# Four edits to a fused attention and expert kernel: transfers and value scaling issued earlier, weight sums on another engine, the last stage's head prepared in the stage before, decay factors computed on the chip

## The chip, the cores and the metric

The kernel runs on one core of a Trainium2 chip. The time is the device time of one execution in microseconds (us). Within the core five engines run side by side, each with its own instruction list in program order: TensorE (PE in the profile), VectorE (DVE), ScalarE (ACT), GpSimd (POOL) and SyncE (SP, which here only issues transfers; ACT issues some as well). Sixteen DMA engines move the data. An engine whose next instruction waits also holds everything that stands behind it in its list.

## The reference, cut to what matters

```python
# attention with a decaying state; B, H, S, D = 4, 8, 768, 64
for t in range(S):
    state = gamma * state + einsum('bhd,bhe->bhde', k[:, :, t], v[:, :, t])
    y[:, :, t] = scale * einsum('bhd,bhde->bhe', q[:, :, t], state)
x = y.transpose(0, 2, 1, 3).reshape(3072, 512)
# first expert block, 512 -> 1024 -> 512
x = ((x @ w1) * (x @ w2)) @ w3 @ w_out
# second expert block, 512 -> 768 -> 512
h = maximum(maximum(x @ u1, x @ u2), x @ u3)
out = h @ u_out
```

The weights are float64 values in memory: the host passes them on as 64-bit words, and the chip decodes them.

## The kernel before, in words

**Attention.** The sequence is cut into 24 chunks of 128 positions (`seq`; two batches take turns, so chunks i and i+2 belong to the same batch, except that chunks 0, 1, 12 and 13 begin a batch and 10, 11, 22 and 23 end one). A chunk is 1 MB, loaded by SP in two halves (`load_half(i, 0)`: q and k by feature; `load_half(i, 1)`: k and v by token) into one of four buffers `ck`, so the load of chunk i+4 can be issued only when chunk i is done with. In iteration i PE does the state product of chunk i (`attn_in`, L311), the scores of chunk i+1 (L303), the value product of chunk i (`attn_av`, L320) and its state update (`attn_st`, L331). POOL multiplies the values by a decay (`scale_v`, L293) before the value product may run. DVE masks the scores into `a` (L304), which the value product reads, and multiplies the result by the output decay `gout` (`attn_ev`, L340), which frees the bank that the state product of chunk i+2 writes. ACT copies the state out of its bank (L335) for the state product of chunk i+2.

**Weights beside it.** Over iterations 2 to 21 a `Spread` deals out jobs, two ticks an iteration: eight weight tiles of 512 KB are decoded, and then `weights` makes seven operands from them. One decode is: transfer into a staging buffer (`fetch`, L85), ACT (L116), POOL (L118), DVE (L139, L141), ACT (L148), DVE (L133). Three transfers are issued by SP in iterations 0 and 1 (`more()`), the other five by ACT, each behind the decode step that frees its staging buffer (`due_more`). `weights` rounds a matrix (ACT, L204), subtracts (DVE, L205), and forms four sums and differences on POOL (L207, L208, L209, L211). The same `weights` prepares operands five more times in the expert stages, once 1024 and four times 768 wide.

**Transfers share eight completion semaphores.** They are handed out in turn, in the order of the program text, whichever engine issues; a transfer is issued only when the one eight before it has landed.

**Expert stages.** Every product is done by a seven-product scheme for 2x2 blocks (`ORDER`, q = 0 to 6), each product with its operand split into a high and a low part (`op_split`, L229 on ACT and L230 on DVE). Stage one (L464 to L466) runs in blocks of seven products; at its third block `wgen(q)` also runs `weights`. The merge (L574 to L576), the stage hj (L694 to L696, 9 blocks) and the last stage (L753 to L755) follow. For the last stage, `quad_o(n)` names the four buffers of block n of its input, `o_load` fills them, `o_pre` forms differences in place (L626 to L631) and `o_split` splits (L639 on ACT, L640 on DVE). Before, hj's last block loads three quarters of block 0 at q = 3 and 5 and the fourth at q = 6 (into `C`, which hj uses until q = 5), splits operand 0 at q = 5, and operand 1 and `o_pre(2)` come behind the stage.

Of the kernel before, what the change touches and what calls it, by code (L numbers as in the profile page):

```python
# [15 lines left out]
P = 128  # L16
B, H, S, D = 4, 8, 768, 64
NP = H // 2
C = 128
# [26 lines left out]
@with_exitstack  # L46
def fused_kernel(ctx: ExitStack, tc: tile.TileContext, ck, w12, w3t, wo1, w123, wo2, mask, gout, kdec, out):
    nc = tc.nc
# [31 lines left out]

    def fetch(src, raw, hi=None, lo=None):
        k = stage_turn[0]
        stage_turn[0] += 1
        st = stg[k % NSTG][:, :]
        (nc.scalar if late[0] else nc.sync).dma_start(out=st.bitcast(I64), in_=src)  # L85
        loaded.append((st, dec_t[k % 2][:, :], raw, hi, lo))
# [3 lines left out]
    def more(k=1):  # L90
        if k > 1:
            due[0] = 0
        for _ in range(k):
            if wq:
                wq.pop(0)()
# [101 lines left out]
    def weights(raw, n, slot=wslot):  # L197
        tmp = s_t[:, :n]

        def emit(q):  # L200
            r0, r1, r2, r3 = raw
            src = (r0, r1, r0, r2, tmp, r3, r1)[q]
            w = slot(q, n)
            nc.scalar.copy(out=w[:, 0], in_=src)  # L204
            nc.vector.tensor_tensor(out=w[:, 1], in0=src, in1=w[:, 0], op=ALU.subtract)  # L205
            if q == 0:
                nc.gpsimd.tensor_tensor(out=tmp, in0=r2, in1=r3, op=ALU.add)  # L207
                nc.gpsimd.tensor_tensor(out=r2, in0=r2, in1=r0, op=ALU.subtract)  # L208
                nc.gpsimd.tensor_tensor(out=r0, in0=tmp, in1=r0, op=ALU.subtract)  # L209
            elif q == 2:  # L210
                nc.gpsimd.tensor_tensor(out=r1, in0=r1, in1=r0, op=ALU.subtract)  # L211

        return emit
# [48 lines left out]
    kdec_sb = a_pl.tile([P, CPB, H], F32, name="kdec")  # L262
    a_pl.tile([P, 8], F32, name="pad_a")

# [42 lines left out]
    def attn_in(i):  # L307
        t, y = cks(i), y_bank(i)
        if seq[i][1]:
            for p in range(NP):  # L310
                nc.tensor.matmul(y[:, p, :], st_sb[i % 2][:, p, :], t[:, 0, p * C:(p + 1) * C],  # L311
                                 start=p == 0, stop=False, skip_group_check=True)
# [30 lines left out]

    def fetch_w12(i, u):
        raw = wraw_t[0][:, :].rearrange("p (q i n) -> p q i n", q=4, i=GA)
        fetch(w12[i, u], raw[:, 2 * u:2 * u + 2, i % GA, :])

# [11 lines left out]
    with tc.manual_schedule():  # L359
        load_half(0, 0)  # L360
        nc.sync.dma_start(out=mask_sb, in_=mask)
        load_half(0, 1)
        nc.sync.dma_start(out=kdec_sb, in_=kdec)
        load_half(1, 0)
        load_half(1, 1)
        nc.sync.dma_start(out=gout_sb[:, 0], in_=gout[:, 0])
        for b in range(2):
            nc.gpsimd.memset(st_sb[b], 0.0)
        wq += [lambda i=i, u=u: fetch_w12(i, u) for i in range(GA) for u in range(2)]
        load_half(2, 0)  # L370
        load_half(2, 1)
        nc.sync.dma_start(out=gout_sb[:, 1:2], in_=gout[:, 1:2])
        load_half(3, 0)
# [8 lines left out]
        side = Spread([step] * (4 * GA) + [drain] + [lambda q=q: wgen(q) for q in (0, 1, 5, 2, 3, 4, 6)], 2 * (last - 3))  # L382
        for i in range(last + 1):
            attn_in(i)
            if i:
                scores(i + 1)
            if i > 1:
                side.tick()
            attn_av(i)
            scale_v(i + 2)  # L390
            attn_st(i)
            if not i:
                scores(i + 1)
            attn_ev(i)
            if i > 1:
                side.tick()
            load_half(i + 4, 0)
            if i < 2:
                more()
                if i == 1:  # L400
                    more()
                    nc.sync.dma_start(out=gout_sb[:, 2:], in_=gout[:, 2:])
            load_half(i + 4, 1)
            if i == last - 2:
                op_split(0, quad_b(0)(0, 0))
# [199 lines left out]
        def quad_o(n):  # L605
            if n % 2:
                raw = (wraw_t[0][:, :1536], wraw_t[0][:, 1536:], m_a[:, :1536], w_t[6][:, :1536].bitcast(F32))
            else:
                raw = [work[nm][:, :1536] for nm in "TEUC"]
            return lambda k, e: raw[2 * e + k]  # L610
# [31 lines left out]
        for j in range(GH):  # L642
# [16 lines left out]
            for n in range(NB):  # L659
# [3 lines left out]
                for q in range(7):  # L663
# [14 lines left out]
                    if j == GH - 1 and n == NB - 1:  # L678
                        if q == 3:
                            o_load(0, 0, 0)  # L680
                            o_load(0, 0, 1)
                        elif q == 5:
                            o_split(0)
                            o_load(0, 1, 0)
                        elif q == 6:
                            o_load(0, 1, 1)
                    which, first = ORDER[q]
# [48 lines left out]
        o_sets = [[bank[k] for k in (2, 3, 0, 1)], bank[4:8]]  # L736
        o_split(1)
        o_pre(2)
        for s in range(7 * NB):
# [92 lines left out]
```

## Time and profile before

| | us |
|---|---|
| median of 3 runs (lowest to highest) | 863.97 (860.59 to 864.65) |
| the profiled execution: its time | 863.8 |
| its span, first to last instruction | 862.0 |
| PE busy | 840.9 (98%) |
| DVE busy | 589.1 (68%) |
| ACT busy | 363.8 (42%) |
| POOL busy | 190.2 (22%) |

How to read it: attention takes the first 102.8 us of the span, the expert stages the rest. A profile row of an instruction group gives its start, its length, the engine, the line, what is written from what, and in brackets how long the engine stood idle before it and what seems to have released it. PE's granted clock was 0.999 of full speed.

### The profile page before, as it was taken

Reading aid. Unit: us, or ns where it says so; the run is one execution under the profiler, and the core shown is the slowest. Engines: PE = TensorE matmul, PEld = TensorE weight load, DVE = VectorE, ACT = ScalarE, POOL = GpSimd, SP = SyncE. Lnnn points to the kernel's source line nnn. Section 1 sums busy time; section 2 is a strip of 40 time slices with the busy share of each in tenths; the row PEclk is TensorE's granted clock in tenths of the full one; section 3 lists DMA queues with packets and bytes.
Section 4 is the critical chain, followed back from the end, with each engine's and each line's share of the span. In section 5 each row is a group of like instructions: output and inputs, shape, how many; then the busy total and the mean of one; then the engine's idle time right before and its main releaser. Section 6 shows DMA issues by size and latency. Waiting matters only on the chain.

```text
span 862.0 us, 12688 instructions
## 1 busy us (share of the span) xinstructions
PE 840.9 (98%) x4938; PEld 716.6 (83%) x4938; DVE 589.1 (68%) x716; ACT 363.8 (42%) x564; POOL 190.2 (22%) x148
## 2 busy tenths in 40 slices
PE   8887999999999999999999999999999999999998
PEld 7877888887888888888888878888888888889998
DVE  2788959899475757663375768677655675688783
ACT  1423453644335353543454444453333344335542
POOL 2437415174130313100110231240003013000000
PEclk9999999999999999999999999999999999999999
DMA  8997467967979886462386599929998899873422
GB/s 331 379 401 263 149 265 263 374 244 277 382 276 357 302 309 251 139 244 97 110 313 261 179 370 400 381 98 367 421 347 306 328 367 329 296 270 145 178 99 99
DMA packets 54781, 236.34 MB, mean 274 GB/s; under 512 B 6208, under 2 KB 6336, under 8 KB 39360
## 3 DMA queue, kind: packets, MB, share of 16 engines
q1 hardware_dynamic: 37440, 132.23, 39.9%
q10 hardware_dynamic: 17280, 103.29, 32.5%
q8 instruction: 39, 0.64, 0.3%
q14 instruction: 22, 0.18, 0.1%
HBM read 163.14 MB, written 72.35 MB: 273 GB/s over the span
## 4 chain that ended last, share of the span: by engine, by line
PE 79%; DMA 8%; DVE 6%; issue 3%; ACT 1%; POOL 1%; SPq 0%; ACTq 0%; POOLq 0%; DVEq 0%
PE bank L694 9%; PE bank L695 8%; PE bank L696 8%; PE bank L465 7%; PE bank L466 7%; PE bank L464 7%; PE bank L576 4%; PE bank L575 4%; PE bank L574 4%; DMA ck<-in_ck_dram 4%; PE bank L755 3%; PE bank L754 3%; PE bank L753 3%; PE bank L515 2%; PE bank L513 2%
## 5 line engine op out<-in xcount | busy, mean ns | idle before, releaser
L694 PE MATMUL bank<-op,w 128*128 128x512 f32 x360 | 140.4, 390 | 0.6 <-ACT U L699 0.3
L696 PE MATMUL bank<-op,w 128*128 128x512 f32 x360 | 140.1, 389 | 0.0
L695 PE MATMUL bank<-op,w 128*128 128x512 f32 x360 | 140.1, 389 | 0.0
L118 POOL TENSOR_SCALAR dec<-dec 128x512 f32<-128x512 f32 x64 | 49.5, 774 | 392.9 <-ACT dec L116 369.4
L465 PE MATMUL bank<-op,w 128*128 128x512 f32 x336 | 130.9, 389 | 1.4 <-DVE op L230 1.4
L464 PE MATMUL bank<-op,w 128*128 128x512 f32 x336 | 130.9, 390 | 0.2 <-DVE U L471 0.2
L466 PE MATMUL bank<-op,w 128*128 128x512 f32 x336 | 130.8, 389 | 0.0
L694 PEld LDWEIGHTS bank<-op,w 128*128 128x128 f32 x360 | 67.6, 188 | 15.9 <-issue 1.3
L696 PEld LDWEIGHTS bank<-op,w 128*128 128x128 f32 x360 | 67.6, 188 | 14.2
L695 PEld LDWEIGHTS bank<-op,w 128*128 128x128 f32 x360 | 67.6, 188 | 13.9
L465 PEld LDWEIGHTS bank<-op,w 128*128 128x128 f32 x336 | 63.1, 188 | 14.9 <-DVE op L230 1.8
L574 PE MATMUL bank<-op,w 128*128 128x512 f32 x192 | 74.7, 389 | 0.0
L575 PE MATMUL bank<-op,w 128*128 128x512 f32 x192 | 74.7, 389 | 0.0
L576 PE MATMUL bank<-op,w 128*128 128x512 f32 x192 | 74.7, 389 | 0.0
L464 PEld LDWEIGHTS bank<-op,w 128*128 128x128 f32 x336 | 63.1, 188 | 13.8 <-issue 0.8
L466 PEld LDWEIGHTS bank<-op,w 128*128 128x128 f32 x336 | 63.1, 188 | 13.1
L148 ACT ACTIVATE dec<-stg 128x512 int32<-128x512 uint32 x64 | 43.0, 671 | 65.9 <-DVE stg L141 60.9
L116 ACT ACTIVATE dec<-stg 128x512 f32<-128x512 f32 x64 | 42.4, 663 | 41.6 <-DMA stg<-in_w_dram 17.5
L755 PE MATMUL bank<-wo,w 128*128 128x256 f32 x192 | 54.4, 283 | 1.0 <-DVE w L640 1.0
L754 PE MATMUL bank<-wo,w 128*128 128x256 f32 x192 | 54.3, 283 | 0.0
L753 PE MATMUL bank<-wo,w 128*128 128x256 f32 x192 | 54.3, 283 | 0.0
L139 DVE TENSOR_SCALAR dec<-dec 128x512 int32<-128x512 int32 x64 | 35.2, 550 | 24.6 <-POOL dec L118 24.6
(177 smaller groups left out, 1646.7 us busy)
## 6 DMA issues: line engine op xcount, KB each, us to landing
op<-opsp ACTq DMA_DIRECT2D x77, 1024.0 KB, 7.7
opsp<-op SPq DMA_DIRECT2D x25, 1024.0 KB, 6.0
ck<-in_ck_dram SPq DMA_DIRECT2D x48, 512.0 KB, 8.7
opsp<-w SPq DMA_DIRECT2D x14, 1024.0 KB, 5.7
stg<-in_w_dram ACTq DMA_DIRECT2D x19, 512.0 KB, 6.4
stg<-in_w3t_dram ACTq DMA_DIRECT2D x16, 512.0 KB, 3.5
hsp<-m SPq DMA_DIRECT2D x32, 256.0 KB, 7.4
stg<-in_w_dram SPq DMA_DIRECT2D x15, 512.0 KB, 9.5
```

The source lines that it names most:

```text
L464: nc.tensor.matmul(ps, wh, x[:, 0, k, :], start=first and k == 0, stop=False, skip_group_check=True)
L465: nc.tensor.matmul(ps, wh, x[:, 1, k, :], start=False, stop=False, skip_group_check=True)
L466: nc.tensor.matmul(ps, wl, x[:, 0, k, :], start=False, stop=k == 1, skip_group_check=True)
L574: nc.tensor.matmul(ps, wh, x[:, 0, k, :], start=kk == 0 and k == 0, stop=False)
L575: nc.tensor.matmul(ps, wh, x[:, 1, k, :], start=False, stop=False)
L576: nc.tensor.matmul(ps, wl, x[:, 0, k, :], start=False, stop=kk == 3 and k == 1)
L694: nc.tensor.matmul(ps, wh, x[:, 0, k, :], start=first and k == 0, stop=False, skip_group_check=True)
L695: nc.tensor.matmul(ps, wh, x[:, 1, k, :], start=False, stop=False, skip_group_check=True)
L696: nc.tensor.matmul(ps, wl, x[:, 0, k, :], start=False, stop=k == 1, skip_group_check=True)
L753: nc.tensor.matmul(ps, xh[:, k, o], wh[:, k], start=first and k == 0, stop=False, skip_group_check=True)
L754: nc.tensor.matmul(ps, xh[:, k, o], wl[:, k], start=False, stop=False, skip_group_check=True)
L755: nc.tensor.matmul(ps, xl[:, k, o], wh[:, k], start=False, stop=k == 2, skip_group_check=True)
```

## The change

Four edits. (1) In attention `scale_v(i + 2)` moves from behind the value product to the head of iteration i; `kdec` and `mask` are loaded by ACT's queue; all eight weight transfers are issued by SP, in iterations 0, 1, 3, 5, 6, 8, 10 and 11, between the two halves of a chunk's load. The first five go into free room in `xr2` (attention writes that tile from iteration 13 on), the others into the three staging buffers. (2) The sums in `weights` run on DVE, and two of them move from q = 0 to q = 1. (3) Block 0 of the last stage gets other buffers, is loaded at q = 3 and 4 of hj's last block, and operand 1 and `o_pre(2)` are done at q = 6 of it. (4) Only the first of six slices of `gout` is loaded (256 KB in place of 1.5 MB), with a small table `gch`; ACT makes the other five by scaling, four instructions a slice.

```diff
-        nc.sync.dma_start(out=mask_sb, in_=mask)
+        nc.scalar.dma_start(out=kdec_sb, in_=kdec)
...
-        nc.sync.dma_start(out=kdec_sb, in_=kdec)
+        nc.scalar.dma_start(out=mask_sb, in_=mask)
...
-        nc.sync.dma_start(out=gout_sb[:, 0], in_=gout[:, 0])
-        wq += [lambda i=i, u=u: fetch_w12(i, u) for i in range(GA) for u in range(2)]
+        room = xr_t[2][:, :, :, :].rearrange("p k e n -> p (k e n)")
+        home = [room[:, z * 1024:z * 1024 + 1024] for z in (0, 1, 2, 3, 0)] + [None] * 3
+        early = [lambda k=k: fetch_w12(k // 2, k % 2, home[k]) for k in range(2 * GA)]
-        nc.sync.dma_start(out=gout_sb[:, 1:2], in_=gout[:, 1:2])
+        nc.sync.dma_start(out=gout_sb[:, 0], in_=gout)
+        nc.sync.dma_start(out=gch_sb, in_=gch)
...
         for i in range(last + 1):
+            scale_v(i + 2)
             attn_in(i)
...
             attn_av(i)
-            scale_v(i + 2)
             attn_st(i)
...
             load_half(i + 4, 0)
-            if i < 2:
-                more()
-                if i == 1:
-                    more()
-                    nc.sync.dma_start(out=gout_sb[:, 2:], in_=gout[:, 2:])
+            if i in (0, 1, 3, 5, 6, 8, 10, 11):
+                early.pop(0)()
+            if i % 2 == 0 and i // 2 + 1 < CPB:
+                for n in range(NP):
+                    nc.scalar.activation(out=gout_sb[:, i // 2 + 1, n], in_=gout_sb[:, 0, n], func=ACT.Copy,
+                                         scale=gch_sb[:, i // 2 + 1, n:n + 1])
             load_half(i + 4, 1)
...
             if q == 0:
-                nc.gpsimd.tensor_tensor(out=tmp, in0=r2, in1=r3, op=ALU.add)
-                nc.gpsimd.tensor_tensor(out=r2, in0=r2, in1=r0, op=ALU.subtract)
-                nc.gpsimd.tensor_tensor(out=r0, in0=tmp, in1=r0, op=ALU.subtract)
+                nc.vector.tensor_tensor(out=tmp, in0=r2, in1=r3, op=ALU.add)
+            elif q == 1:
+                nc.vector.tensor_tensor(out=r2, in0=r2, in1=r0, op=ALU.subtract)
+                nc.vector.tensor_tensor(out=r0, in0=tmp, in1=r0, op=ALU.subtract)
             elif q == 2:
-                nc.gpsimd.tensor_tensor(out=r1, in0=r1, in1=r0, op=ALU.subtract)
+                nc.vector.tensor_tensor(out=r1, in0=r1, in1=r0, op=ALU.subtract)
...
-                raw = [work[nm][:, :1536] for nm in "TEUC"]
+                raw = (work["T"][:, :], wraw_t[0][:, 1536:], work["U"][:, :1536], wraw_t[0][:, :1536])
...
+                        elif q == 4:
+                            o_load(0, 1, 0)
+                            o_load(0, 1, 1)
                         elif q == 5:
                             o_split(0)
-                            o_load(0, 1, 0)
                         elif q == 6:
-                            o_load(0, 1, 1)
+                            o_split(1)
+                            o_pre(2)
...
-        o_split(1)
-        o_pre(2)
```

**Place 1, SP in the middle of attention.** Before, SP's list holds only the loads of the chunks there (`ck_97` to `ck_99` and `ck_96` are the four buffers); the names behind "waits" are the semaphores of transfers (DMAHW) and engines. The weight transfers stand in ACT's list.

```order
L274 DMA ck_96<-in_ck_dram 128x1024 [waits DMAHW2_49,PE_49,Pool_49]
L274 DMA ck_97<-in_ck_dram 128x1024 [waits DMAHW3_49,PE_49]
L274 DMA ck_97<-in_ck_dram 128x1024 [waits DMAHW5_49,PE_49,Pool_49]
L274 DMA ck_98<-in_ck_dram 128x1024 [waits DMAHW6_49,DMAHW4_49,PE_49]
L274 DMA ck_98<-in_ck_dram 128x1024 [waits DMAHW7_49,PE_49,Pool_49]
```

Now, from the load of the same chunk on (`xr_95` is the room in `xr2`):

```order
L276 DMA ck_96<-in_ck_dram 128x1024 [waits DMAHW0_49,PE_49,Pool_49]
L276 DMA ck_97<-in_ck_dram 128x1024 [waits DMAHW1_49,PE_49]
L85 DMA xr_95<-in_w_dram 128x512 [waits DMAHW2_49]
L276 DMA ck_97<-in_ck_dram 128x1024 [waits DMAHW3_49,PE_49,Pool_49]
L276 DMA ck_98<-in_ck_dram 128x1024 [waits DMAHW4_49,PE_49]
L85 DMA xr_95<-in_w_dram 128x512 [waits DMAHW5_49,DVE_49]
L276 DMA ck_98<-in_ck_dram 128x1024 [waits DMAHW6_49,PE_49,Pool_49]
```

Before, the third row waits for semaphore 5, which the fourth weight transfer carries, issued from ACT's list; now the weight transfers stand in SP's own list, and the eighth transfer before any of these is one that SP issued itself.

**Place 2, DVE in iterations 15 to 17.** `w_65`, `w_66`, `w_70` and `w_67` are the first operands that `weights` makes, `wraw` the decoded matrix, `a` and `xr` the mask's and the decay's outputs. Before:

```order
L304 TENSOR_TENSOR a_101<-pair_84,mask 128x1024
L205 TENSOR_TENSOR w_65<-wraw,w_65 128x1024
L340 TENSOR_TENSOR xr_94<-abank_85,gout 128x8x64
L304 TENSOR_TENSOR a_100<-pair_83,mask 128x1024
L205 TENSOR_TENSOR w_66<-wraw,w_66 128x1024
L340 TENSOR_TENSOR xr_95<-abank_86,gout 128x8x64
L205 TENSOR_TENSOR w_70<-wraw,w_70 128x1024
```

Now:

```order
L306 TENSOR_TENSOR a_101<-pair_84,mask 128x1024
L205 TENSOR_TENSOR w_65<-wraw,w_65 128x1024
L207 TENSOR_TENSOR s_t<-wraw 128x1024
L342 TENSOR_TENSOR xr_94<-abank_85,gout 128x8x64
L306 TENSOR_TENSOR a_100<-pair_83,mask 128x1024
L205 TENSOR_TENSOR w_66<-wraw,w_66 128x1024
L209 TENSOR_TENSOR wraw<-wraw 128x1024
L210 TENSOR_TENSOR wraw<-s_t,wraw 128x1024
L342 TENSOR_TENSOR xr_95<-abank_86,gout 128x8x64
L205 TENSOR_TENSOR w_70<-wraw,w_70 128x1024
```

One sum stands ahead of iteration 16's decay, two ahead of iteration 17's.

**Place 3, POOL in iterations 2 and 3.** `ck_96` is chunk 4, `ck_97` chunk 5; L118 is the decode of the first and second weight tile. Before:

```order
L293 TENSOR_TENSOR ck_99<-ck_99,kdec 128x512
L118 TENSOR_SCALAR dec_63<-dec_63 128x512
L293 TENSOR_TENSOR ck_96<-ck_96,kdec 128x512
L118 TENSOR_SCALAR dec_64<-dec_64 128x512
L293 TENSOR_TENSOR ck_97<-ck_97,kdec 128x512
```

Now:

```order
L295 TENSOR_TENSOR ck_99<-ck_99,kdec 128x512
L295 TENSOR_TENSOR ck_96<-ck_96,kdec 128x512
L118 TENSOR_SCALAR dec_63<-dec_63 128x512
L118 TENSOR_SCALAR dec_64<-dec_64 128x512
L295 TENSOR_TENSOR ck_97<-ck_97,kdec 128x512
```

The decode step of the first tile now stands behind the scaling of chunk 4. The fourth and the seventh tile's step move behind one scaling in the same way; the other five keep their place.

## Rows read from the trace of the kernel before

**Rows 1.** Waits of PE over the span: who, total us, times, longest

```profile
PE abank L320 <- POOL ck L293: 5.2, 4, 1.8
PE pair L303 <- DMA ck<-in_ck_dram: 4.3, 5, 1.3
PE abank L311 <- ACT dec L148: 1.8, 2, 0.9
PE bank L465 <- DVE op L230: 1.4, 1, 1.4
PE abank L311 <- ACT st L335: 1.2, 1, 1.2
PE bank L755 <- DVE w L640: 1.0, 1, 1.0
```

**Rows 2.** Timeline of PE: chunk 4's state product, one iteration, attention's end

```profile
24.43 1.13 PE L311 MATMUL abank<-ck,st 128*128 128x128 f32 x8 [0.91 <-ACT dec L148]
...
73.10 1.16 PE L311 MATMUL abank<-ck,st 128*128 128x128 f32 x8
74.19 1.16 PE L303 MATMUL pair<-ck 64*128 64x128 f32 x16
75.28 1.09 PE L320 MATMUL abank<-a,ck 128*64 128x128 f32 x16
76.20 0.63 PE L331 MATMUL abank<-ck 128*64 128x64 f32 x16
76.77 1.16 PE L311 MATMUL abank<-ck,st 128*128 128x128 f32 x8
...
102.81 0.50 PE L464 MATMUL bank<-op,w 128*128 128x512 f32 x1
```

**Rows 3.** SP's waits, its timeline from 36 us, POOL's waits

```profile
SPq L274 <- DMA stg<-in_w_dram: 8.8, 3, 7.1
...
36.76 1.93 SPq L274 DMA_DIRECT2D ck<-in_ck_dram  x4
...
POOL ck L293 <- DMA ck<-in_ck_dram: 15.4, 7, 3.3
```

**Rows 4.** Windows: busy us (instructions) of PE, PEld, DVE, ACT, POOL; clock, DMA share, GB/s

```profile
28.00:36.00 8.00, 6.74 (x100) 6.05 (x96) 5.16 (x8) 3.40 (x7) 3.59 (x4) 1.00 1.03 418
36.00:48.00 12.00, 12.00 (x194) 11.01 (x189) 10.10 (x14) 4.34 (x10) 5.01 (x6) 1.00 0.92 317
```

**Rows 5.** Timeline of ACT, DVE and PE around the last weight tile

```profile
66.28 0.66 ACT L116 ACTIVATE dec<-stg 128x512 f32<-128x512 f32 x1 [3.48 <-DMA stg<-in_w_dram]
...
70.30 1.21 DVE L304 TENSOR_TENSOR a<-pair,mask 128x1024 f32<-128x1024 f32 x1
...
71.61 1.09 PE L320 MATMUL abank<-a,ck 128*64 128x128 f32 x16 [1.58 <-POOL ck L293]
```

**Rows 6.** Timeline of POOL at chunk 4's scaling

```profile
21.94 1.20 POOL L293 TENSOR_TENSOR ck<-ck,kdec 128x512 f32<-128x512 f32 x1 [0.16 <-POOL dec L118]
```

**Rows 7.** Timeline of POOL and DVE in the weight phase

```profile
76.37 2.36 POOL L208 TENSOR_TENSOR wraw<-wraw 128x1024 f32<-128x1024 f32 x1
...
76.54 3.27 DVE L205 TENSOR_TENSOR w<-wraw,w 128x1024 fp32r<-128x1024 f32 x1
...
97.60 1.21 DVE L205 TENSOR_TENSOR w<-wraw,w 128x1024 fp32r<-128x1024 f32 x1
```

**Rows 8.** Timeline of DVE in stage one's third block

```profile
199.67 3.42 DVE L230 TENSOR_TENSOR op<-xr,op 128x1024 fp32r<-128x1024 f32 x1
```

**Rows 9.** Timeline of DVE at the head of the last stage

```profile
765.24 0.69 DVE L714 TENSOR_TENSOR m<-m,C 128x512 f32<-128x512 f32 x1
765.85 1.47 DVE L706 TENSOR_TENSOR m<-m,bank 128x512 f32<-128x512 f32 x2
...
772.90 1.75 DVE L629 TENSOR_TENSOR U<-C,U 128x1536 f32<-128x1536 f32 x1
774.57 1.75 DVE L640 TENSOR_TENSOR w<-m,w 128x1536 fp32r<-128x1536 f32 x1
```

More of the change, by code (lines that the diff above doesn't have):

```diff
@@ L46, in fused_kernel @@
 @with_exitstack
-def fused_kernel(ctx: ExitStack, tc: tile.TileContext, ck, w12, w3t, wo1, w123, wo2, mask, gout, kdec, out):
+def fused_kernel(ctx: ExitStack, tc: tile.TileContext, ck, w12, w3t, wo1, w123, wo2, mask, gout, gch, kdec, out):
     nc = tc.nc
@@ L79, in fused_kernel, with fetch @@
     loaded, fronts, pending, wq = [], [], [], []
-    def fetch(src, raw, hi=None, lo=None):
+    def fetch(src, raw, hi=None, lo=None, st=None):
         k = stage_turn[0]
         stage_turn[0] += 1
-        st = stg[k % NSTG][:, :]
+        st = stg[k % NSTG][:, :] if st is None else st
         (nc.scalar if late[0] else nc.sync).dma_start(out=st.bitcast(I64), in_=src)
@@ L262, in fused_kernel @@
     kdec_sb = a_pl.tile([P, CPB, H], F32, name="kdec")
-    a_pl.tile([P, 8], F32, name="pad_a")
+    gch_sb = a_pl.tile([P, CPB, NP], F32, name="gch")
+    a_pl.tile([P, 16], F32, name="pad_a")
     seq = [(2 * g + z, j) for g in range(2) for j in range(CPB) for z in range(2)]
@@ L342, in attn_ev, with fetch_w12 @@
                                 in1=gout_sb[:, j].rearrange("p n (e t) -> p n e t", e=2), op=ALU.mult)
-    def fetch_w12(i, u):
+    def fetch_w12(i, u, st=None):
         raw = wraw_t[0][:, :].rearrange("p (q i n) -> p q i n", q=4, i=GA)
-        fetch(w12[i, u], raw[:, 2 * u:2 * u + 2, i % GA, :])
+        fetch(w12[i, u], raw[:, 2 * u:2 * u + 2, i % GA, :], st=st)
     def fetch_w123(j, w, u):
@@ L606, in quad_o @@
             if n % 2:
-                raw = (wraw_t[0][:, :1536], wraw_t[0][:, 1536:], m_a[:, :1536], w_t[6][:, :1536].bitcast(F32))
+                raw = (work["C"][:, :1536], work["E"][:, :1536], m_a[:, :1536], w_t[6][:, :1536].bitcast(F32))
             else:
-                raw = [work[nm][:, :1536] for nm in "TEUC"]
+                raw = (work["T"][:, :], wraw_t[0][:, 1536:], work["U"][:, :1536], wraw_t[0][:, :1536])
             return lambda k, e: raw[2 * e + k]
@@ L806 @@
         "mask": t[None, tp] >= t[:, None],
-        "gout": np.repeat(gout.reshape(NP, 2, 1, CPB, C), D, axis=2).transpose(1, 2, 3, 0, 4).reshape(P, CPB, NP, C),
+        "gout": np.repeat(gout.reshape(NP, 2, 1, CPB, C), D, axis=2).transpose(1, 2, 3, 0, 4).reshape(P, CPB, NP, C)[:, 0],
+        "gch": np.repeat((g[None, :] ** (C * np.arange(CPB, dtype=np.float64))[:, None]).reshape(CPB, NP, 2).transpose(2, 0, 1), D, axis=0),
         "kdec": kdec.transpose(1, 0, 2),
@@ L826 @@
     out = nc.dram_tensor("out_0_dram", (NT, DM), F32, kind="ExternalOutput").ap()
-    names = ("ck", "w12", "w3t", "wo1", "w123", "wo2", "mask", "gout", "kdec")
+    names = ("ck", "w12", "w3t", "wo1", "w123", "wo2", "mask", "gout", "gch", "kdec")
     with tile.TileContext(nc) as tc:
```

## The prediction, made before the run

> **What bounds the kernel now.** I read PE's waits first. PE is busy 98% of the span, so a change that removes no product can only take away waits of PE, and the view lists them by what ended them: POOL's scaling 5.2 us, chunk loads 4.3, ACT 1.8 and 1.2, all on attention's lines, and one wait each of 1.4 (stage one) and 1.0 (last stage) [rows 1]. The expert stages hide nearly everything; attention does not.
>
> Next I read PE's timeline in attention. An undisturbed iteration is 3.67 us (73.10 to 76.77): state product 1.09, scores 1.09, value product 0.92, state update 0.57 [rows 2]. From chunk 4's state product at 24.43 to attention's end at 102.81 it takes 78.4 us [rows 2]. The work in it is 18 state products, 19 scores, 16 value products with update (1.49) and 4 without (about 1): 19.6 + 20.7 + 23.8 + 4 = 68.1 us. So 10.3 us are waits. The same count from 76.77 (iteration 17) on is 7 x 1.09 + 6 x 1.09 + 5 x 1.49 + 2 = 23.6 of 26.0 us. So 7.9 us of waits lie between 24 and 77 us, and 2.4 after it, where the weight operands are made.
>
> Then I asked who is late. SP once waited 7.1 us for a weight transfer and issued nothing until 36.76 [rows 3]: that transfer stood in ACT's list, was issued late, and a chunk load eight places behind it could not go before it had landed. The windows show the hole: 418 GB/s from 28 to 36 us, 317 from 36 to 48 [rows 4]. Some 12 us x 100 GB/s = 1.2 MB are missing, about 2.9 us of transfer, and with four chunk buffers PE meets that debt after 50 us, where the chunks without state product or update go by faster. The other kind is the late weight tile itself: ACT waited 3.48 us for the last one until 66.28, DVE's mask for chunk 15 stood behind that tile's decode and ended at 71.5, and PE went on at 71.61 [rows 5]. The wait is booked on POOL, but the instruction that ended last is DVE's.
>
> **The change, part by part.** The profiled execution (863.8 us, span 862.0) carries the sum; it is 0.2 below the median, so no correction.
>
> *The first 24 us.* The small loads leave SP's list, the scaling comes earlier, and 0.25 MB less of `gout` lies ahead of the loads. But chunk 4's state product waits for chunk 2's decay, which stands on DVE behind the first tile's decode. POOL now scales chunk 4 first, while before that scaling stood behind L118 and went at 21.94 without having waited for its load [rows 6]; it puts one scaling (1.0 to 1.2) ahead of L118. The bounds are 1.2 lost and the 0.9 of that wait [rows 2] gained; I take 0, since both ends are alike.
>
> *Weight transfers on SP, less gout.* Eight transfers of 512 KB, as many as before, each issued from SP's own list about two iterations (7 us) ahead of its first use; the last of them goes out with iteration 11, while before it was issued late enough that ACT waited for it until 66.28, in iteration 14 [rows 5]. And 1.25 MB of `gout` (3.0 us at 418 GB/s [rows 4]) is gone. What is queued behind each is the other half of a chunk's load; SP does not stop, since rooms and staging buffers are free. From the chunk loads alone, plus the eight transfers, 29.7 MB at 418 GB/s are 71 us, well ahead of PE's 102.8. So the 7.9 us should go, except what reappears as single waits on ACT or DVE. ACT's 20 scalings of 128x128 lie in an engine that is a third busy here (4.34 of 12 us [rows 4]). Upper bound 7.9; lower bound 3.0, if only the bytes count. I take 7.4, near the upper end, because the rows show both kinds of wait behind the same late issue.
>
> *Scaling earlier.* This covers what remains of POOL's waits; three of eight L118 move behind a scaling, and POOL waited for chunk loads in 7 places, 15.4 us in all [rows 3]. With loads in time I price it at 0; the price without that cover is a rival below.
>
> *Sums on DVE in attention.* Four sums of 1024 leave POOL (2.4 us each [rows 7]) for DVE, 1.21 each, the length of L205 on the same shape when POOL is still [rows 7]; successive starts on DVE lie 0.08 closer than the lengths (1.75 long, 1.67 apart [rows 9]), so 1.13. DVE's work in iterations 16 to 21 becomes: six masks (1.13 by their 1.21 [rows 5]), six decays (about 0.6, the distance of a 128x512 operation of 0.69 from the next [rows 9]), seven L205, four sums and one split, 6.8 + 3.6 + 7.9 + 4.5 + 1.1 = 23.9 us, against 22.0 of PE. Iteration 17 is the heavy one (6.2 of DVE in 3.67). Before, L205 took 3.27 while a POOL sum ran beside it and 1.21 without [rows 7], so the 4.5 us are about what the stretches cost. A mask has 1.4 us to spare (scores end to value product 2.6, less 1.2). Bounds: 0.7 of waits (the chain with DVE to itself) and about 6 (each of six remaining scalings, 1.04, also blocks DVE: 6.2 more, less what is spare). Against 2.4 now that is a gain of 1.7 or a loss of 3.6. I take 2.2, a gain of 0.2.
>
> *Sums in stage one's third block.* The split that PE waited 1.4 us for is a DVE operation of 3.42 us [rows 1, 8] that is 1.21 elsewhere; it is the last of three such operations ahead of the wait, each about 2.1 longer beside POOL's sums. Three sums now stand ahead of it, 3 x 1.13 = 3.4, and 3 x 2.1 = 6.4 fall away: 3.0 earlier, so the wait is gone. Gain 1.4; bounds 1.4 gained and 3.4 lost if the stretch has another cause. In the four other uses (768 wide) the sums are hidden under products, on an engine with idle time before the next eviction: 0.
>
> *The last stage's head.* PE waited 1.0 for operand 2's low part, which ended at 774.57 + 1.75 = 776.3. Now, behind hj's eviction that ends at 765.9, DVE has operand 1, two differences, the two evictions of q = 6 (1.4), a difference and operand 2: 5 x 1.67 + 0.1 + 1.4 = 9.8, so 775.7 [rows 9]. Before, it had the same work plus a stop for the load of `C`. Gain 0.6; bounds 1.0 gained, and 0.6 lost if a load lands late.
>
> Sum: 0 + 7.4 + 0.2 + 1.4 + 0.6 = 9.6, so 863.8 - 9.6 = **854.2 us**.
>
> **The rivals.**
>
> *Only the bytes count.* The list that issues a transfer changes nothing of the data stream, and the holes between 36 and 48 us have another cause. For it: the DMA engines' share stays at 0.92 in that window while the rate falls [rows 4]. Against it: SP's stop of 7.1 us [rows 3]. Then only 3.0 of the 7.9 go: 863.8 - 3.0 - 0.2 - 1.4 - 0.6 = 858.6 us. The Trainium skill (DMA: Bandwidth & Descriptors, section Issuing engines are not separate DMA queues) has a rule that points there: transfers from any issuing engine end on the same 16 DMA engines and interleave, so moving them only saves the sequencer's time to issue. By that rule the move is worth nothing in rate; the trace differs in that the issue itself was late, which the rule does not speak of.
>
> *DVE becomes the bound (the other side).* The sums put 8 x 1.13 + 16 x 0.87 = 23 us on DVE (0.87 for 768 columns, estimated from 1.13 for 1024). If the stretches are not POOL's doing, nothing is given back: attention's 4.5, stage one's 4.5 and the 3.5 of hj's first change of weights come through to PE, 12.5 against 9.6 gained, and the result is 866.7 us. It decides when more than 9.6 of the 23 us are uncovered. For it: DVE's share of busy time from 36 to 48 us is already 84% [rows 4]. Against it: the 3.27 and 3.42 of operations that take 1.21. A half of it, the upper bound in attention alone (3.6 + 0.2 lost), ends at 858.0.
>
> *Scaling in front holds the decode.* Three L118 stand behind a scaling that waits for its load; if those loads come a full iteration late, 3.67 - 1.4 = 2.3 us reach PE each time, 7 in all: 861.2 us. For it: the 15.4 us [rows 3]. Against it: those loads were late for the cause that goes.
>
> **How the numbers follow.** Forecast as summed, 851 to 857.5: 0.62. Only the bytes, or the half of DVE's rival: 0.17, faster still. Scaling in front, or most terms lost: 0.13, within 0.5%. DVE the bound, 866.7: 0.08. A measurement of this kernel tells about 0.5% (4.3 us) from no change, so faster means below 859.7. Faster 0.79, same 0.13, slower 0.08. The low end takes all upper bounds: 0.9 + 7.9 + 1.7 + 1.4 + 1.0 = 12.9, 851.0. The high end takes in the bytes alone and stops at 860.5, short of 861.2, which leaves some 0.2 outside. Likeliest point 854.2.
>
> **What would show it.** In the new profile: attention's end near 95.2 (102.8 - 7.4 - 0.2); no SP wait above some 4 us for a weight transfer and no window of 317 GB/s while loads are due; PE's waits for chunk loads after 24 us gone; L205 and the splits near 1.2 in the weight phases; PE's 1.4 in stage one gone, the last stage's 1.0 cut by half. Wrong would be: PE waiting for DVE's mask or decay in iterations 17 to 20 by several us, PE waiting in stage one's third block, or chunk 4's state product later than 25.5.

## The result and the profile after

| | before | after |
|---|---|---|
| median, us (lowest to highest, runs) | 864.31 (860.59 to 864.97, 4) | 855.07 (854.41 to 855.94, 4) |
| ratio of the times, 95% interval | | 0.9904 (0.9884 to 0.9924) |
| profiled execution: time, span | 863.8, 862.0 | 854.41, 852.6 |

The change made the kernel 9.2 us (1.0%) faster; the forecast was 854.2. The page's first part shows the work moved as planned: POOL fell from 190.2 to 131.6 us, and PE is still busy 98%.

```profile
span 852.6 us, 12700 instructions
PE 838.6 (98%) x4938; PEld 716.4 (84%) x4938; DVE 594.0 (70%) x740; ACT 370.1 (43%) x584; POOL 131.6 (15%) x124
```

PE's waits over the whole span, which answer to [rows 1]. All waits for chunk loads (4.3) and for POOL's scaling (5.2) are gone, and so are the two of the expert stages (1.4 and 1.0). What took their place is smaller: 3.4 booked on ACT's decode (1.8 before), 3.9 called "issue" (0.5 before), and 1.4 on DVE's output decay, which is new. The 1.3 for L369, at the start of the program, stood there before as well.

```profile
PE abank L322 <- issue: 3.9, 5, 1.4
PE abank L313 <- ACT dec L148: 3.4, 2, 1.8
PE abank L313 <- DVE xr L342: 1.4, 1, 1.4
PE abank L380 <- POOL st L369: 1.3, 1, 1.3
PE bank L703 <- DVE op L231: 0.2, 1, 0.2
```

PE's timeline after, at the places of [rows 2]: chunk 4's state product, the late weight tile, iteration 17's state product and three waits behind it, attention's end.

```profile
23.76 1.13 PE L313 MATMUL abank<-ck,st 128*128 128x128 f32 x8 [1.79 <-ACT dec L148]
...
59.23 1.13 PE L313 MATMUL abank<-ck,st 128*128 128x128 f32 x8 [1.59 <-ACT dec L148]
...
70.21 1.16 PE L313 MATMUL abank<-ck,st 128*128 128x128 f32 x8
...
79.06 1.13 PE L313 MATMUL abank<-ck,st 128*128 128x128 f32 x8 [1.44 <-DVE xr L342]
...
86.13 1.09 PE L322 MATMUL abank<-a,ck 128*64 128x128 f32 x16 [1.11 <-issue]
...
96.59 1.09 PE L322 MATMUL abank<-a,ck 128*64 128x128 f32 x16 [0.75 <-issue]
97.61 0.50 PE L469 MATMUL bank<-op,w 128*128 128x512 f32 x1
```

Stage by stage, from the starts of these products in both traces:

| stretch | before | after | gained | forecast |
|---|---|---|---|---|
| start to chunk 4's state product | 24.43 | 23.76 | 0.7 | 0 |
| to iteration 17's state product | 52.3 | 46.45 | 5.9 | 7.4 |
| to attention's end | 26.0 | 27.4 | -1.4 | 0.2 |
| stage one | 230.8 | 228.6 | 2.2 | 1.4 |
| stage hj | 258.6 | 257.9 | 0.7 | 0 |
| last stage | 95.7 | 94.4 | 1.3 | 0.6 |

The products between stage one and hj, the merge among them, take 174.1 us in both traces. The gains sum to 9.4, the difference of the spans. So the sum of 9.6 came out right while attention gave 5.2 instead of 7.6 and the expert stages 4.2 instead of 2.0.

The issuing side answers to [rows 3]: SP waits for chunk loads only 2.4 us in all and for no weight transfer in attention. POOL's waits for chunk loads doubled from 15.4 to 34.2 us, since the scaling now comes up earlier, on an engine without the sums. None of PE's waits in the list above is for a scaling any more; the earlier scaling costs where a decode step stands behind it.

```profile
SPq L276 <- PE abank L333: 34.8, 17, 2.3
...
SPq L276 <- DMA ck<-in_ck_dram: 2.4, 3, 0.9
```

```profile
POOL ck L295 <- DMA ck<-in_ck_dram: 34.2, 17, 5.0
```

The windows of [rows 4] after (same columns). The hole of 317 GB/s is gone: the rate is even, at 384 and 373, and what SP waits for is PE, which frees the chunk buffers (34.8 us above).

```profile
28.00:36.00 8.00, 8.00 (x119) 7.26 (x120) 7.39 (x10) 4.30 (x10) 2.74 (x3) 1.00 1.02 384
36.00:48.00 12.00, 12.00 (x186) 10.95 (x188) 10.17 (x12) 8.52 (x21) 4.48 (x5) 1.00 0.99 373
```

**Where attention fell short: iteration 17.** The timeline of DVE after, then that of POOL:

```profile
73.98 1.21 DVE L205 TENSOR_TENSOR w<-wraw,w 128x1024 fp32r<-128x1024 f32 x1
75.11 1.22 DVE L209 TENSOR_TENSOR wraw<-wraw 128x1024 f32<-128x1024 f32 x1
76.36 1.95 DVE L210 TENSOR_TENSOR wraw<-s_t,wraw 128x1024 f32<-128x1024 f32 x1
78.23 0.68 DVE L342 TENSOR_TENSOR xr<-abank,gout 128x512 f32<-128x512 f32 x1
...
82.83 2.06 DVE L212 TENSOR_TENSOR wraw<-wraw 128x1024 f32<-128x1024 f32 x1
84.81 1.21 DVE L306 TENSOR_TENSOR a<-pair,mask 128x1024 f32<-128x1024 f32 x1
```

```profile
75.84 1.39 POOL L295 TENSOR_TENSOR ck<-ck,kdec 128x512 f32<-128x512 f32 x1 [2.61 <-DMA ck<-in_ck_dram]
...
82.15 1.66 POOL L295 TENSOR_TENSOR ck<-ck,kdec 128x512 f32<-128x512 f32 x1 [1.21 <-DMA ck<-in_ck_dram]
```

Three weight operations of DVE stand ahead of the output decay L342, which frees the bank for the state product of 79.06. L210 takes 1.95 in place of 1.22, because POOL's scaling is under way when it starts (until 77.23). The same happens to the last sum, L212: 2.06 beside the scaling that ends at 83.81, with the mask L306 behind it, and PE waits at 86.13, a wait that the view books on "issue". The Trainium skill (SBUF — State Buffer, section SBUF: two separate sides) says that VectorE with two operands from SBUF and GpSimd hold a shared port pair in turn, each for a whole instruction, not by halves. Both rows agree: 77.23 - 76.36 = 0.87 and 83.81 - 82.83 = 0.98 of blocking, plus 1.08 each, is what they took. A third operation, the L205 at 86.55, took 1.94 beside a scaling, with no wait of PE behind it.

**Where the start fell short: chunk 4.** ACT after, then POOL and DVE:

```profile
18.73 0.67 ACT L116 ACTIVATE dec<-xr 128x512 f32<-128x512 f32 x1 [3.25 <-DMA xr<-in_w_dram]
```

```profile
20.14 1.04 POOL L295 TENSOR_TENSOR ck<-ck,kdec 128x512 f32<-128x512 f32 x1 [2.73 <-DMA ck<-in_ck_dram]
21.15 0.61 POOL L118 TENSOR_SCALAR dec<-dec 128x512 f32<-128x512 f32 x1
```

```profile
21.80 0.43 DVE L139 TENSOR_SCALAR dec<-dec 128x512 int32<-128x512 int32 x1 [3.72 <-POOL dec L118]
...
22.93 0.68 DVE L342 TENSOR_TENSOR xr<-abank,gout 128x512 f32<-128x512 f32 x1
```

ACT's step of the first tile began at 18.73 and took 0.67, but POOL stood at the scaling of chunk 4, waiting for its load. L118 came at 21.15, DVE's decode after it, and the decay of chunk 2, which frees the bank for the state product of 23.76, behind that. This wait of 1.79 is booked on ACT's L148 (23.05 to 23.72), a decode step whose output the product does not read. Of the instructions that it does need, the last to end is DVE's L342, at 23.61.

In stage one's third block the stretch is gone, as an answer to [rows 8] shows (DVE, after); operand 2's low part at the last stage's head, 774.57 in [rows 9], starts at 764.79, 6.6 us into that stage in place of 8.3:

```profile
199.31 1.22 DVE L231 TENSOR_TENSOR op<-xr,op 128x1024 fp32r<-128x1024 f32 x1
...
764.79 1.75 DVE L645 TENSOR_TENSOR w<-m,w 128x1536 fp32r<-128x1536 f32 x1
```

### The profile page after: what moved, and what is told of

It is laid out like the page before. It is cut to its first block, busy times and chain, and to the rows that moved or that the text cites. A ratio compares the mean times of both kernels' runs of the same rounds, so it can differ in the third digit from the quotient of the medians.

```text
span 852.6 us, 12700 instructions
## 1 busy us (share of the span) xinstructions
PE 838.6 (98%) x4938; PEld 716.4 (84%) x4938; DVE 594.0 (70%) x740; ACT 370.1 (43%) x584; POOL 131.6 (15%) x124
## 4 chain that ended last, share of the span: by engine, by line
PE 91%; DVE 4%; DMA 3%; issue 1%; ACT 0%; POOL 0%; SPq 0%; DVEq 0%; POOLq 0%; ACTq 0%
PE bank L703 10%; PE bank L702 10%; PE bank L704 10%; PE bank L469 9%; PE bank L470 9%; PE bank L471 9%; PE bank L581 5%; PE bank L579 5%; PE bank L580 5%; PE bank L761 4%; PE bank L760 4%; PE bank L759 4%; DMA ck<-in_ck_dram 2%; PE bank L520 2%; PE bank L518 2%; PE bank L519 2%
## 5 line engine op out<-in xcount | busy, mean ns | idle before, releaser
L118 POOL TENSOR_SCALAR dec<-dec 128x512 f32<-128x512 f32 x64 | 47.9, 748 | 468.1 <-ACT dec L116 398.6
L148 ACT ACTIVATE dec<-stg 128x512 int32<-128x512 uint32 x59 | 39.5, 670 | 58.0 <-DVE stg L141 54.1
L116 ACT ACTIVATE dec<-stg 128x512 f32<-128x512 f32 x59 | 39.1, 662 | 31.2 <-DMA stg<-in_wo_dram 15.5
```

## The experiments

Each kernel is the changed one with the edit shown, unless another is named. They ran in three groups, each on one chip with the kernel before beside it: e1 to e4 (before: 862.54), e5 to e8 (863.98), e9 and e10 (863.78). The changed kernel ran with a fourth set, beside 864.31. Since these medians differ by up to 1.8 us, a median that lies less than about 1.8 us from the 855.07 settles nothing across groups. There the traces are compared, and e1 to e3 with e4 on their own chip: e4 took 855.03, as after did.

| kernel | median (range, runs) | ratio to before (95%) | span | attention's end |
|---|---|---|---|---|
| after | 855.07 (854.41 to 855.94, 4) | 0.9904 (0.9884 to 0.9924) | 852.6 | 97.6 |
| e1_sums_pool | 856.37 (855.2 to 858.43, 6) | 0.9919 (0.9899 to 0.9939) | 854.5 | 95.15 |
| e2_scale_late | 853.26 (852.72 to 853.52, 6) | 0.9878 (0.9858 to 0.9898) | 851.7 | 96.8 |
| e3_w_on_act | 858.36 (856.1 to 861.91, 7) | 0.994 (0.9917 to 0.9963) | 854.8 | 99.8 |
| e4_gout_full | 855.03 (854.55 to 855.93, 6) | 0.9901 (0.9883 to 0.992) | 852.7 | 97.7 |
| e5_head_undone | 854.25 (853.29 to 855.36, 6) | 0.9892 (0.9873 to 0.9911) | 853.1 | 97.7 |
| e6_only_w_sp | 859.81 (857.2 to 861.75, 9) | 0.995 (0.9932 to 0.9968) | 857.2 | 99.2 |
| e7_neither | 862.2 (859.71 to 864.54, 12) | 0.9984 (0.9971 to 0.9998) | 857.9 | 102.5 |
| e8_sums_split | 853.13 (851.69 to 853.75, 6) | 0.9876 (0.9855 to 0.9896) | 851.4 | 96.3 |
| e9_tile_first | 851.48 (850.79 to 852.0, 4) | 0.9857 (0.9837 to 0.9878) | 850.2 | 94.75 |
| e10_both | 850.35 (849.78 to 850.47, 4) | 0.9845 (0.9829 to 0.9862) | 848.6 | 94.0 |

**e1: the sums back on POOL, everywhere.**

```diff
-                nc.vector.tensor_tensor(out=tmp, in0=r2, in1=r3, op=ALU.add)
-            elif q == 1:
-                nc.vector.tensor_tensor(out=r2, in0=r2, in1=r0, op=ALU.subtract)
...
+                nc.gpsimd.tensor_tensor(out=tmp, in0=r2, in1=r3, op=ALU.add)
+                nc.gpsimd.tensor_tensor(out=r2, in0=r2, in1=r0, op=ALU.subtract)
```

> The changed kernel with the four sums of the weight step back on POOL, all else as changed. Theory (the sums on DVE gain in stage one, where PE's wait and its restarts fell away, 2.2 us, and lose in attention, where iteration 17 became too heavy for DVE, about 1.4): 855.9 us, 0.8 above the changed kernel's 855.1; PE's wait of about 1.4 in stage one's third block is back, attention ends near 96.5 instead of 97.6. Rival (moving the sums to DVE only costs): 852 to 853 us.

The median moved by only 1.3 us (against e4, on the same chip, too), because two effects of opposite sign cancel in it; the trace shows both. Attention ends at 95.15, 2.5 us earlier than after, and from iteration 17 on PE waits only twice. Stage one takes 230.8 again and hj 258.6, with the old wait back:

```profile
PE bank L469 <- DVE op L230: 1.4, 1, 1.4
```

So the sums on DVE cost 2.5 us in attention and bring 2.2 + 0.7 in the expert stages. The 0.7 of hj is near what traces differ by: hj takes 258.2 to 258.6 in the three with the sums on POOL there (before, e1, e6) and 257.5 to 258.0 in the nine others. (The last stage's 95.9 here has another cause, see e5.)

**e2: the scaling back behind the value product.**

```diff
-            scale_v(i + 2)
             attn_in(i)
...
             attn_av(i)
+            scale_v(i + 2)
             attn_st(i)
```

> The changed kernel with the scaling of the values back behind the value product. Theory (the earlier scaling adds nothing once loads come in time, and it puts chunk 4's scaling ahead of the first tile's decode): PE's wait of 1.8 before chunk 4's state product shrinks to about 0.8, 854.3 us. Rival (the earlier scaling is what took POOL's waits away): PE waits again for POOL between 50 and 90 us, 857 to 859 us.

Faster than the changed kernel, by 1.8 us in the medians and 0.8 at attention's end. On its own chip it is 1.8 below e4 as well, and the two ranges do not meet. Chunk 4's product comes 0.4 earlier than after, and the stretch from iteration 18's product to attention's end takes 23.1 in place of 23.7. Near 58 us it is no better: a wait for POOL is back, as the rival had it, and with it PE waits 1.04 + 0.87 there in place of 1.59. Timeline of PE in e2:

```profile
23.35 1.13 PE L313 MATMUL abank<-ck,st 128*128 128x128 f32 x8 [1.26 <-ACT dec L148]
...
56.60 1.09 PE L322 MATMUL abank<-a,ck 128*64 128x128 f32 x16 [1.04 <-POOL ck L295]
...
59.03 1.13 PE L313 MATMUL abank<-ck,st 128*128 128x128 f32 x8 [0.87 <-ACT dec L148]
```

**e3: the weight transfers as before, three from SP and five from ACT; e4: the whole decay table loaded.**

```diff
-        early = [lambda k=k: fetch_w12(k // 2, k % 2, home[k]) for k in range(2 * GA)]
+        wq += [lambda i=i, u=u: fetch_w12(i, u) for i in range(GA) for u in range(2)]
...
-            if i in (0, 1, 3, 5, 6, 8, 10, 11):
-                early.pop(0)()
+            if i < 2:
+                more()
+                if i == 1:
+                    more()
```

```diff
-        nc.sync.dma_start(out=gout_sb[:, 0], in_=gout)
-        nc.sync.dma_start(out=gch_sb, in_=gch)
+        nc.sync.dma_start(out=gout_sb[:, 0], in_=gout[:, 0])
+        nc.sync.dma_start(out=gout_sb[:, 1:2], in_=gout[:, 1:2])
...
+            if i == 1:
+                nc.sync.dma_start(out=gout_sb[:, 2:], in_=gout[:, 2:])
```

> The changed kernel with the weight transfers as before: three on SP in iterations 0 and 1, five on ACT behind the decode. Theory (the order of issue is what mattered): SP again waits some 5 us or more for a weight transfer, PE again waits for chunk loads and late tiles, 859 us. Rival (only the bytes of the decay table count): no change, 855 to 855.5 us.

> The changed kernel with the whole decay table loaded (1.5 MB in three transfers) in place of made by ACT. Theory (transfers run ahead of PE once they are issued in time, so 3 us of bytes are mostly hidden): 855.5 us, at most 1 above the changed kernel. Rival (only the bytes count): 858 us, with PE waiting for chunk loads in the first 35 us.

The transfers are worth 3.3 us in the medians (e4 and e3, on one chip) and 2.2 at attention's end. PE's waits for chunk loads, which the theory expected, did not come back; PE waits 3.0 for scalings and 2.4 for a decay. Part of the 3.3 goes with TensorE's clock: e3's three runs with a mean granted clock of 0.998 or more have a median of 856.5, the four at 0.995 to 0.997 took 858.4 to 861.9. The 1.25 MB less of table, with the transfers in their new place, are worth nothing (855.03 against 855.07, attention's end 0.1 apart); that is net of ACT's scalings, which e4 leaves out as well. SP's wait for a weight transfer is back in e3, halved:

```profile
SPq L276 <- DMA stg<-in_w_dram: 4.4, 3, 3.3
```

**e5: the last stage's head as before.**

```diff
-                raw = (work["T"][:, :], wraw_t[0][:, 1536:], work["U"][:, :1536], wraw_t[0][:, :1536])
+                raw = [work[nm][:, :1536] for nm in "TEUC"]
...
-                            o_split(1)
-                            o_pre(2)
+                            o_load(0, 1, 1)
...
+        o_split(1)
+        o_pre(2)
```

> The changed kernel with the last stage's head as before (buffers, loads at q = 3, 5 and 6, operand 1 behind the stage). Theory (the move took away a wait of 1.0 us and PE's slow restart after it): PE's wait at the head is back, 856.3 us. Rival (the head hangs on the landing of the first load, which differs from run to run, so the move gives nothing steady): 855.1 us, no wait or a wait in both.

No loss in the medians (854.25, where 856.3 was expected), and 95.0 for the last stage against 94.4, with a wait that is new against after:

```profile
PE bank L760 <- DVE w L645: 0.4, 1, 0.4
```

The other traces bear the 0.6 out: with the old head the last stage takes 95.0 to 95.7 (e5, e6, before), with the new one 94.4 to 94.8 in eight of nine. The ninth is e1, with 95.9 and waits of 0.6 and 0.4. There the first load, whose issue the edit does not touch, came late: issued at 740.3 in both e1 and after, it had landed by 748.5 in the trace of after and at 752.4 in that of e1. What sets that landing time was not tried.

**e6: the kernel before, with the weight transfers alone moved to SP.**

```diff
+        room = xr_t[2][:, :, :, :].rearrange("p k e n -> p (k e n)")
+        home = [room[:, z * 1024:z * 1024 + 1024] for z in (0, 1, 2, 3, 0)] + [None] * 3
...
+            if i in (0, 1, 3, 5, 6, 8, 10, 11):
+                early.pop(0)()
+            if i == 1:
+                nc.sync.dma_start(out=gout_sb[:, 2:], in_=gout[:, 2:])
```

> The kernel before with one edit: all eight weight transfers issued by SP in iterations 0 to 11. Theory (the order of issue bounds the middle of attention): SP waits no longer for weight transfers, the windows from 36 to 48 us carry some 370 GB/s or more, attention ends near 98.5 in place of 102.8, 859 us. Rival (only the bytes count): 862 to 864 us, as the kernel before.

It moves the same bytes as before from another list: 4.2 us faster in the medians, 3.6 at attention's end, and the rate from 36 to 48 us is 414 where it was 317 [rows 4]. SP waits for a weight transfer no longer than 0.2 us there. Two things change with the list: five tiles go into the room in `xr2`, and the last four transfers go out 0.6 to 4.6 us earlier than before (the first four at the same time or later). What the room alone would bring, with five transfers left in ACT's list, was not tried.

```profile
36.00:48.00 12.00, 10.49 (x154) 9.62 (x156) 11.22 (x13) 4.79 (x10) 5.57 (x6) 1.00 1.03 414
```

**e7: e3 and e4 together** (their two diffs).

> The changed kernel with both undone that lighten the transfers: weight transfers as before, and the decay table loaded in full. Alone they cost 3.3 us and 0. Theory (they are substitutes: either one clears the debt that PE meets after 50 us): together they cost more than their sum, 860.5 us, SP's long wait for a weight transfer is back at 6 us or more. Rival (independent costs that add): 858.4 us.

7.1 us slower than after in the medians, though e3 and e4 apart cost 3.3 and 0; at attention's end 4.9 against 2.2 and 0.1. So the two act as substitutes, as the theory had it: late transfers hurt most when the table's bytes stand in the way as well, and with the transfers in time the table is hidden. SP's waits and the windows of e7:

```profile
SPq L275 <- DMA stg<-in_w_dram: 13.7, 5, 6.3
```

```profile
36.00:48.00 12.00, 11.97 (x181) 10.85 (x181) 8.91 (x13) 5.47 (x12) 4.74 (x5) 1.00 0.90 302
...
56.00:58.00 2.00, 0.74 (x8) 0.78 (x10) 2.00 (x4) 0.12 (x1) 0.47 (x1) 0.75 1.03 420
58.00:60.00 2.00, 2.00 (x28) 1.90 (x24) 1.48 (x2) 0.67 (x1) 0.03 (x1) 0.50 1.02 416
```

Some 1.5 us of e7's 4.9 are another loss: the granted clock fell behind a wait of PE (last section). Without them 3.4 are left, still more than 2.2 + 0.1, though these are single executions. The clock is in the medians too: its mean was below 0.998 in six of e7's twelve runs and in none of after's and e4's. e7's other six have a median of 861.2, which is 6.2 above after, where e3's runs of that kind are 1.4 above it; so the clock alone does not make the excess.

**e8: attention's sums on POOL, the five later uses on DVE.**

```diff
+            if pool_sums:
+                if q == 0:
+                    nc.gpsimd.tensor_tensor(out=tmp, in0=r2, in1=r3, op=ALU.add)
...
-        wgen = weights(raw_quads(1024), 1024)
+        wgen = weights(raw_quads(1024), 1024, pool_sums=True)
```

> The changed kernel with the sums of attention's weight step on POOL, those of the five later uses on DVE. Theory (in attention DVE is the one that is late, so the sums cost there; in the expert stages POOL's sums block DVE's operations): attention ends near 95.1 as with all sums on POOL, and the expert stages stay at 755.0, 852.6 us. Rival (the earlier end was chance, or is given back at the next stage): 855 us.

853.13: the expert stages keep what DVE gave them (755.1 of span behind attention's end, 755.0 after, 759.35 in e1), and from iteration 18's state product to attention's end it takes 21.2 us (after 23.7, e1 21.1). Attention still ends 1.2 later than in e1, since the clock fell behind the wait for chunk 4 in this trace and cost 1.5 (last section). The product itself starts as in e1 (24.05 and 24.00; 23.76 after), with the same code at that place. The waits ahead of it, 2.88, 2.40 and 1.79, differ more than these starts, because PE was done with the work before it at different times.

**e9: e8, with chunk 4's scaling behind the first tile's decode step.**

```diff
-            scale_v(i + 2)
+            if i != 2:
+                scale_v(i + 2)
             attn_in(i)
...
                 side.tick()
+            if i == 2:
+                scale_v(i + 2)
             attn_av(i)
```

> As the split of the sums (853.1 us), with chunk 4's scaling alone moved behind the first tick of iteration 2, so that POOL clamps the first weight tile before it waits for chunk 4's load. Theory (what holds chunk 4's state product is the order on POOL: the tile is there 1.4 us before the load, and POOL, DVE and PE pass that on): the wait of 2.9 us at 24 us shrinks to about 1.1, 851.4 us. Rival (the first 24 us hang on transfers whatever the order): the product still starts at 24, 853.1 us.

851.48. On POOL the decode step now goes first (timelines of PE, then of POOL), and the state product of chunk 4 follows at 23.22 with 1.04 of waiting. With the scaling first it starts between 23.76 and 24.14 (after, e1, e3, e4, e5, e7, e8), with the decode step first at 23.35, 23.22 and 22.82 (e2, e9, e10), so the order on POOL is a cause of it.

```profile
23.22 1.13 PE L320 MATMUL abank<-ck,st 128*128 128x128 f32 x8 [1.04 <-ACT dec L148]
```

```profile
19.95 0.61 POOL L118 TENSOR_SCALAR dec<-dec 128x512 f32<-128x512 f32 x1 [2.22 <-ACT dec L116]
20.62 1.30 POOL L302 TENSOR_TENSOR ck<-ck,kdec 128x512 f32<-128x512 f32 x1
```

**e10: e9, with the last two weight transfers one iteration earlier.**

```diff
-            if i in (0, 1, 3, 5, 6, 8, 10, 11):
+            if i in (0, 1, 3, 5, 6, 8, 9, 10):
```

> As the run before this one, and the last two weight transfers one iteration earlier (9 and 10 in place of 10 and 11). Theory (the wait of 1.3 us near 60 us is the seventh tile landing late): that wait goes, 850.2 us. Rival (chunk loads are then late by the same bytes): the wait changes its name, 851.4 us or more.

850.35, the fastest version: 13.4 below the kernel before on its chip. The wait of the late tile near 59 us (1.28 at 58.12 in e9) is gone, and the largest left in attention is one of 1.57 for a scaling near 79 us. PE's waits in e10:

```profile
PE abank L329 <- issue: 2.1, 2, 1.4
PE abank L329 <- POOL ck L302: 2.0, 2, 1.6
...
PE abank L320 <- ACT dec L148: 0.3, 1, 0.3
```

## Why the prediction was right, and where it was not

*The time.* Right to 0.9 us, and the likeliest case ("as summed") happened. But attention came out 2.4 short of its terms and the expert stages 2.2 above theirs; that the two errors cancel is luck.

*Weight transfers on SP, less gout (7.4 of 7.9).* The mechanism holds: e6 gains 4.2 with no byte saved (in its trace the stretch of this term gains 4.0), and SP's waits and the hole of 317 GB/s go with it. Too large by 1.5: 5.9 came, and the missing part is the one late tile near 59 us (1.59), of the kind that the text allowed for as "single waits on ACT or DVE", but at 0.5. e10 shows that an earlier issue takes it away. "Only the bytes count" falls by e6 and e4: in e6 the rate went from 317 to 414 with the same bytes, because SP no longer stood behind a transfer of ACT's list. The rule of the Trainium skill that the prediction set against the trace (DMA: Bandwidth & Descriptors, section Issuing engines are not separate DMA queues) says that issuing from several engines at once only saves the sequencer's time. It is not refuted by this, since here the list decided when transfers were issued at all; but whoever took the edit to be worth nothing by it would have missed 4.2 us. Bytes are not free either: e7 shows that they matter once the issue is late.

*Sums on DVE in attention (a gain of 0.2, bounds +1.7 and -3.6).* The term that failed: -1.4 in the stretch, and -2.5 from the sums alone (e1). The step was "the 4.5 us are about what the stretches cost". The total was about right (DVE was busy for 24.3 us in iterations 16 to 21 of the trace after, 23.9 in the sum), but PE does not wait for a total: iteration 17 puts two sums and an L205 in a row ahead of the decay, and POOL's scalings, which stay, lengthen them (1.95 and 2.06 for 1.22). The loss of 3.6 at the lower bound named this mechanism, for six scalings; three of them lengthened an operation of DVE, and PE waited behind two.

*Sums in stage one's third block (1.4).* The wait went as worked out; 2.2 came. Most of the 0.8 that was not in the sum is how a wait is counted: PE's products start 0.23 apart in that block, and the wait that the view gives as 1.4 is a gap of 1.75 before, followed by one of 0.34, so it costs 1.6. A second stop, of 0.2 by the view at 195.83, costs 0.4 in the same way. Both gaps are gone after. PE before:

```profile
201.39 0.39 PE L464 MATMUL bank<-op,w 128*128 128x512 f32 x1
203.14 0.50 PE L465 MATMUL bank<-op,w 128*128 128x512 f32 x1 [1.36 <-DVE op L230]
```

*The other four sums (0)*: 0.7 in hj, which e1 gives back and the other traces bear out (see e1).

*Scaling earlier (0), with the first 24 us (0).* The start gained 0.7, inside its bounds; chunk 4 still waits 1.79, for the very order on POOL that "one scaling (1.0 to 1.2) ahead of L118" described. Without the earlier scaling the start gains 1.1 (e2: 23.35), so that order costs 0.4; the 1.1 come from the small loads on ACT's queue, the smaller table and the moved weight transfers together, and the small loads were not tried alone (e4, with the whole table, starts 0.2 later than after). Over all of attention the earlier scaling is a loss: e2 is 0.8 faster in the trace, and 1.8 below e4 on one chip. "Scaling in front holds the decode" was thus real at one place, chunk 4, where L118 came 1.75 us after its input was ready (21.15 against 18.73 + 0.67), and not at 2.3 us three times; the late tile of 59.23 is not of this kind, since its L118 (55.97) waited for ACT and ACT for the transfer, not behind a scaling.

*The last stage's head (0.6).* 0.6 between the traces of e5 and after, and about as much between the old head and the new one over all traces but e1's; nothing in the medians, which cannot show so little across chips. The stage itself gained 1.3 from before to after, so half of that is not shown to be the move; the first load lands 8.2 us after its issue in one trace (after) and 12.1 in another (e1).

*"DVE becomes the bound"*, at a chance of 0.08, came true in one stretch of attention (PE's waits at 79.06 and 86.13) and nowhere else.

Of the signs named ahead, SP's waits, the windows, the chunk loads and the two expert waits came as told; attention's end did not (97.6, not 95.2), and the splits were near 1.2 in stage one's third block (but for an L205 of 2.00 beside another operation of POOL), while in attention three operations of DVE took 1.94 to 2.06. A sign of being wrong came in part: PE waited 1.44 for DVE's decay and 1.11 for its mask in iterations 19 and 20.

## What to carry to other kernels

When several engines' lists share completion semaphores in program order, a transfer issued late from one list stops the other lists behind it; look for a wait of the issuing engine with a dip of the rate, and issue early from the list that must not stop. Before moving work to another engine, do not go by its share of busy time alone; list what stands there in front of the next instruction that PE needs, iteration by iteration. The sums on DVE cost 2.5 us in attention, where they stood ahead of what PE waited for, and brought 2.9 in the expert stages, where POOL's sums had lengthened DVE's operations; splitting them by use took both gains. A load-dependent instruction at the head of an in-order list delays everything behind it, so put what is ready first.

## What the runs showed of the hardware

The granted clock of TensorE fell to its lower level behind a wait in three of the profiled runs: after 2.88 us idle at 24 us in e8, 2.40 at 79.65 in e5, and 0.91 and then 2.01 near 55 us in e7. The timeline of PE in e8, then the windows (the columns of [rows 4]):

```profile
24.05 1.28 PE L320 MATMUL abank<-ck,st 128*128 128x128 f32 x8 [2.88 <-ACT dec L148]
25.25 2.08 PE L312 MATMUL pair<-ck 64*128 64x128 f32 x16
27.27 1.58 PE L329 MATMUL abank<-a,ck 128*64 128x128 f32 x16
...
29.24 1.16 PE L320 MATMUL abank<-ck,st 128*128 128x128 f32 x8
```

```profile
24.00:26.00 2.00, 1.95 (x14) 1.76 (x16) 2.00 (x3) 1.98 (x7) 1.35 (x2) 0.72 1.03 414
26.00:28.00 2.00, 2.00 (x22) 1.78 (x20) 1.91 (x3) 0.50 (x2) 1.31 (x2) 0.50 1.03 412
```

0.50 is the level of 1.2 GHz. The iteration took 29.24 - 24.05 = 5.2 us in place of 3.67, so a wait of 2.9 cost 4.4. It does not follow every such wait: in e1 PE was idle 2.40 at the same place, in e3 2.40 at 82.36, and the clock stayed at 1.00. Of e8's six runs, the three with a mean granted clock of 0.998 took 853.5 us on average and the three at 1.000 took 852.3, which fits one fall in the former; that each of them fell at this place is not shown. e9, whose wait is shorter, showed no such fall in its trace. Of the 1.65 us that it gains on e8 in the medians, part is thus the clock: in the traces e9's product of chunk 4 starts 0.8 earlier, the next one 2.4 earlier, some 1.5 of it by the clock, and 0.8 is lost again at 79.84, where e9 waits 1.16 for a scaling and e8 only 0.4. Against e8's three runs at 1.000 the gain is 0.8.
